# Layer 1's last two token blocks: seven block products for 12 of 16 inner slices, and a joined sign in the first weight steps

## The chip, the cores and the metric

The kernel runs on one core of one Trainium2 chip. The time is device microseconds of one execution. TensorE (PE) does the matmuls, VectorE (DVE), ScalarE (ACT) and GpSimd (POOL) the rest, and SyncE (SP) issues most DMAs.

## What is computed

Three independent things in one launch: an attention over 4 x 8 heads with 576 tokens (a coarse part over groups of four tokens and a local part under a band mask), and two layers over 2304 tokens each, chained so that the attention's output feeds layer 1 and layer 1's output feeds layer 2:

```python
out = out_up + out_local                     # attention, 2304 tokens x 512
h = np.maximum(x @ w_in, 0.0)                # layer 1: w_in 512 x 2048
y = h * h @ w_out                            #          w_out 2048 x 512
h = x @ w_in                                 # layer 2
g = np.maximum(h, 0.0) + np.log1p(np.exp(-np.abs(h)))
y = g @ w_out
```

All values are float32. PE is fed values rounded to a shorter format, so every operand is kept as a high part and a rest (`xh`, `xl` for the input, `gh`, `gl` for the activation, the two halves of `w` for the weights), and a product is three matmuls: high by high, high by rest, rest by high.

## The kernel before

**Tiles and steps.** Tokens come in five blocks of 512, 384, 384, 512 and 512. The inner dimension of 2048 is cut into 16 slices of 128. A step is (layer, block, slice): its hidden part is 12 matmuls (four pieces of the input dimension by three products) into a bank `ph` (L1315), the activation runs on ACT (`activate`; for layer 1 `Relu` and `Square`, L1328 and L1331; for layer 2 `Abs`, `Exp`, `Ln` on ACT and one DVE instruction, L1339), DVE and ACT split it into `gh` and `gl`, and the output part is 12 matmuls into four banks `y` (L1389), which collect all slices of a block.

**Order of the steps.** `RUNS` lists them by (layer, block, slices). Blocks 0 to 2 go through both layers while the attention of later blocks is still computed beside them. Then come `(0, 3, ALL), (0, 4, ALL[::-1])`, layer 1 of blocks 3 and 4, with a plain hidden part for each, and at last layer 2 of these two blocks, in another form.

**Seven products.** In layer 2 the hidden parts of blocks `ONE` = 3 and `TWO` = 4 for two slices are computed together as a 2 x 2 block product (Strassen's scheme): the two halves of the input dimension, the two slices, the two blocks. `fast_hidden` issues seven products `p` of 6 matmuls each (L1258) where the plain form has 4 x 12 = 48. The scheme needs sums of inputs (`token_sums`, `more_sums`, `last_sums`, split into `tt` or into block `TWO`'s own `xh`, `xl` by `t_split`), sums of weights (`weight_sums`: two sums `wf` of 512 columns, four of 256, one cast and two rests `ws` per pair), and sums of products (`keep_sum` copies a bank to `sum` on ACT, `add_sum` adds a bank to it on DVE at L1285, which also frees the bank). The banks that hold products are two of the ring `r_h` and two of the ring `r_a`. Block `TWO`'s activations are kept in `stash` until its outputs run.

**Weights.** Eight slots hold a slice's weights. The first time, SP loads raw words (`raw<-wts`, a ring of three) and `weight_job` (L425 to L462) turns 8-byte words into high part and rest: ACT takes the absolute value (L433), the low limb (L437) and the signed high limb (L439), DVE shifts and masks (L444), adds (L447, `f<-f,r`), one of both casts, and DVE takes the rest (L375). A slice needed again is loaded ready-made from `wdram` by POOL (L477).

**What sets the order.** The kernel is built by a planner: each strand of work is a generator that yields an engine, a duration and the events it needs, and the class `Order` always issues the one that can start first, with an urgency to break ties. What an engine does is then in that fixed order. Where the planner sees PE idle in the first part, `idle` matmuls on `ident` (L1068) are issued as fillers.

Of the kernel before, what the change touches and what calls it, by code (L numbers as in the profile page):

```python
# [44 lines left out]
LOW, HIGH = list(range(NF // 2)), list(range(NF // 2, NF))  # L45
ALL = LOW + HIGH
KEEP = 5
RUNS = [(0, 0, LOW), (0, 1, ALL), (0, 0, HIGH), (1, 1, HIGH), (1, 0, HIGH + LOW), (1, 1, LOW[:KEEP]),
        (0, 2, ALL), (1, 1, LOW[KEEP:]), (1, 2, LOW[KEEP:] + HIGH + LOW[:KEEP]),
        (0, 3, ALL), (0, 4, ALL[::-1])]  # L50
XBUF = [0, 1, 0, 1, 0]
ONE, TWO = 3, 4
PAIRS = [(f, f + 1) for f in range(0, NF, 2)]
# [18 lines left out]
UNIT_STEPS = [[0, 0] for _ in PAIRS]  # L72
for i, fs in ((ONE, [(0, 0), (1, 0), (0, 1), (1, 1)] + [(u, k) for u in range(2, len(PAIRS)) for k in range(2)]),
              (TWO, [(u, k) for u in reversed(range(len(PAIRS))) for k in (1, 0)])):
    FIRST[i + NB] = start = len(STEPS)
    for u, k in fs:
        if i == ONE:
            UNIT_STEPS[u][k] = len(STEPS)
        halves = ((0, 256), (256, 256)) if i == TWO and (u, k) == fs[-1] else ((0, 512),)
        for t0, n in halves:  # L80
            RUN_OF.append((start, PAIRS[fs[-1][0]][fs[-1][1]]))
            STEPS.append((1, i, PAIRS[u][k], t0, n))
    LAST[i + NB] = len(STEPS) - 1
FAST_TWO = FIRST[TWO + NB]
# [14 lines left out]
OUTS = 4  # L99
# [11 lines left out]
def plan_weights():  # L111


    uses = [lay * NF + f for lay, _, f, _, _ in STEPS]
    held, fills, fill_of, used = {}, [], [], {}
    for s, c in enumerate(uses):
        if c not in held:
            free = [i for i in range(SLOTS) if i not in held.values()]
            if free:
                held[c] = free[0]  # L120
            else:
                near = uses[max(0, s - (5 if s >= FAST else 3)):s]

                def worth(x):
                    return -min(uses.index(x, s) if x in uses[s:] else len(uses), s + NF + 1), used[held[x]]

                old = min((x for x in held if x not in near), key=worth)
                held[c] = held.pop(old)
            fills.append((s, c, held[c], used.get(held[c])))
        used[held[c]] = s  # L130
        fill_of.append(max(i for i, x in enumerate(fills) if x[1] == c))
    return fills, fill_of
# [39 lines left out]
class Ring:  # L172
# [10 lines left out]
    def take(self, name):  # L183
        b = Event()
        b.tile, b.free = self.make(name), None
        self.taken.append(b)
        return b

# [115 lines left out]
def fused_kernel(ctx: ExitStack, tc: tile.TileContext, lq, lk, lv, dqk, dv, cdmask, pqk, pv, pvn, wts, cmask, cident, out):  # L304
    nc = tc.nc
    act, dve, pe, sp = nc.scalar, nc.vector, nc.tensor, nc.sync
    const = ctx.enter_context(tc.tile_pool(name="const", bufs=1))
# [12 lines left out]
    ident = const.tile([128, 128], F32, name="ident")  # L320
    fours = const.tile([128, 32], F32, name="fours")
    placed = const.tile([128, 224], F32, name="placed")
    mask = const.tile([128, 3, KW], F32, name="mask")
    ident16 = const.tile([128, 128], BF16, name="ident16")
    mask16 = const.tile([128, 3, KW], BF16, name="mask16")
# [4 lines left out]
    r_r = ring(prep, "r", [128, 512], 2, I32)  # L330
    r_xh = [ring(main, f"xh{k}", [128, NP, NMAX], 1, F32R) for k in range(2)]
    r_xl = [ring(main, f"xl{k}", [128, NP, NMAX], 1, F32R) for k in range(2)]
    r_part = ring(prep, "part", [128, NMAX], NP)
# [63 lines left out]
    jobs = [(i, half) for i in range(len(fills)) for half in range(2) if half or fills[i][0] < FAST_TWO]  # L397
# [27 lines left out]
    def weight_job(j):  # L425
# [11 lines left out]
        act.activation(out=limbs[:, :, 0], in_=low, func=AF.Copy, scale=2.0 ** -13)  # L437
        t = yield "act", t_act(512)
        act.activation(out=limbs[:, :, 1].bitcast(I16), in_=high.bitcast(F32), func=AF.Prelu,  # L439
                       scale=2.0 ** -19, alpha=2.0 ** 60)  # L440
        raw.free = t
# [3 lines left out]
                          op0=ALU.logical_shift_left, op1=ALU.bitwise_and)  # L445
        t = yield "dve", t_dve(512)
# [17 lines left out]
    def slot_free(j):  # L464
        (_, _, slot, old), half = fills[j[0]], j[1]
        needs = [lent[slot]] if slot in lent else []
        if old is not None:
            needs.append((hidden_done, out_done)[half][old])
# [611 lines left out]
    whole, two_y = events(NP), events(NP)  # L1080
    plain = {(i, m): Event() for i in (ONE, TWO) for m in range(NP)}
    t_ready = {(n, kk): Event() for n in range(1, 5) for kk in range(2)}
    stashed = {x: Event() for x in range(NF)}

    def open_late():
# [10 lines left out]
        late.at = 0.0  # L1096
        for kk in range(2):
            order.spawn(token_sums(kk), FAST - 30)
        for u in range(len(PAIRS)):
            order.spawn(weight_sums(u), UNIT_STEPS[u][0] + U_WEIGHTS)  # L1100

    def pass_late(i, m, y):

        if i == TWO:
            two_y[m].buf = y
            yield None, 0.0
            two_y[m].at = order.free["pe"] + 0.1
            return
        t = yield either, t_either(512), late, late_ring
        b = whole[m].buf = late.stash.take("xf")  # L1110
        copy(b.tile, y.tile)
        y.free = whole[m].at = t
        yield from plain_split(i, m, b.tile)

    def plain_split(i, m, x):

        t = yield either, t_either(512, i == ONE)
# [4 lines left out]
        plain[i, m].at = t + 0.1  # L1122
        if i == TWO:
            two_y[m].buf.free = t
# [7 lines left out]
    def token_sums(kk):  # L1132

        t = yield "dve", t_dve(512), whole[kk], two_y[kk], late_ring
        t1 = late.stash.take("t1")
        dve.tensor_tensor(out=t1.tile, in0=two_y[kk].buf.tile, in1=whole[kk].buf.tile, op=ALU.subtract)
        two_y[kk].buf.free = t
        order.spawn(t_split(1, kk, t1), FAST - 28, t)
        order.spawn(more_sums(kk, t1), FAST - 26.5, t)

    def more_sums(kk, t1):

        t = yield "dve", t_dve(512), whole[kk + 2], two_y[kk + 2], late_ring
        t2, y = late.stash.take("t2"), two_y[kk + 2].buf
        dve.tensor_tensor(out=t2.tile, in0=y.tile, in1=t1.tile, op=ALU.subtract)
        order.spawn(t_split(2, kk, t2), FAST - 24, t)
        order.spawn(plain_split(TWO, kk + 2, y.tile), FAST - 19, t)
        order.spawn(last_sums(kk, t2), FAST - 20, t)

    def last_sums(kk, t2):  # L1150

        for n, op in ((3, ALU.subtract), (4, ALU.subtract)):
            t = yield "dve", t_dve(512), late_ring
            b = late.stash.take("t3")
            x, y = (t2, whole[kk].buf) if n == 3 else (whole[kk + 2].buf, t2)
            dve.tensor_tensor(out=b.tile, in0=x.tile, in1=y.tile, op=op)
            order.spawn(t_split(n, kk, b), FAST - 21 if n == 3 else FAST - 18, t)
        whole[kk].buf.free = whole[kk + 2].buf.free = t

    def t_split(n, kk, b):  # L1160

        th, tl = t_tiles(n, kk)
        t = yield "act", t_act(512)
# [3 lines left out]
        t_ready[n, kk].at = b.free = t + 0.1  # L1167

    def weight_sums(u):

        s0, s1 = UNIT_STEPS[u]
# [21 lines left out]
        s_ready[u].buf = b  # L1193
        s_ready[u].at = t + 0.1

    s_ready, ending = events(len(PAIRS)), events(2)
# [9 lines left out]
    def fast_hidden():  # L1206

        order.late = True
        units = [Event() for _ in PAIRS]
        for u, x in enumerate(units):  # L1210
            x.copied, x.added = events(3), Event()
            x.sums = [None] * 3
        seq = [(u, p) for ps in ((1, 2), (5,), (6,), (7,), (4,), (3,)) for u in range(2) for p in ps] + [(2, 1)]
        for u in range(2, len(PAIRS)):
            seq += [(u, 2), (u, 6), (u, 5), (u, 7)] + [(u + 1, 1)] * (u < len(PAIRS) - 1) + [(u, 4), (u, 3)]
        first, second = ([x.tile for x in x_tiles[i].buf] for i in (ONE, TWO))
        for u, p in seq:
            x, (s0, s1) = units[u], UNIT_STEPS[u]
            w0, w1 = (weights[fills[fill_of[s]][2]][:, 0] if w_ready[fill_of[s], 0].at is not None else None
                      for s in (s0, s1))  # L1220
            ones = [plain[ONE, kk + 2 * (p == 2)] for kk in range(2)]
            needs = {1: [r_h, w_ready[fill_of[s0], 0], *ones], 2: [r_a, w_ready[fill_of[s0], 0], *ones],
                     6: [x.copied[0], s_ready[u], t_ready[2, 0], t_ready[2, 1]],
                     5: [r_a, s_ready[u], t_ready[1, 0], t_ready[1, 1]],
                     7: [x.copied[1], s_ready[u], t_ready[3, 0], t_ready[3, 1]],
                     4: [x.copied[2], w_ready[fill_of[s1], 0], t_ready[4, 0], t_ready[4, 1]],
                     3: [x.added, s_ready[u], plain[TWO, 2], plain[TWO, 3]]}[p]
            if (u, p) == (1, 1):
                needs.append(out_done[FAST - 1])
            t = yield "pe", 6 * t_pe(512), *needs  # L1230
            w0, w1 = (weights[fills[fill_of[s]][2]][:, 0] for s in (s0, s1))
            if u == len(PAIRS) - 1 and p in (3, 7):
                ending[p == 3].at = t - 0.1
            if p == 1:
                x.long = r_h.take("p1")
                hidden_at[s0].at = hidden_at[s1].at = t
            elif p == 2:
                x.b = r_a.take("p2")
            elif p == 5:
                x.d = r_a.take("p5")  # L1240
            bank = {2: x.__dict__.get("b"), 5: x.__dict__.get("d"), 3: x.__dict__.get("d")}.get(p, x.long)
            prs = []
            for kk in range(2):
# [3 lines left out]
                else:  # L1247
                    k = SUMS[{6: 2, 5: 1, 7: 3, 3: 4}[p]] + kk * 128
                    a, c = (s_ready[u].buf.tile[:, half, k:k + 128] for half in range(2))
# [11 lines left out]
            if p in (1, 6, 7):  # L1261
                order.spawn(keep_sum(x, (1, 6, 7).index(p)), s0 - 20 if u > 1 else FAST - 29, at)
            if p == 2:
                order.spawn(add_sum(x, 0, x.b, s0, None, True), s0 - 20 if u > 1 else FAST - 27 + u, at)
# [339 lines left out]
```

## Time and profile before

| | us |
|---|---|
| median of 3 runs | 887.42 (886.86 to 889.75) |
| profiled execution | 886.4 |
| its span, first to last instruction | 884.6 |
| busy: PE, DVE, ACT, POOL | 875.5, 660.1, 508.5, 80.9 |
| layer 1, blocks 3 and 4 | 539.19 to 712.67 |
| layer 2's phase of seven products | 712.67 to 829.05 |
| outputs of the last block | 829.05 to 880.7 |

Times in rows are counted from the span's start. A matmul's duration in a row is longer than its share of PE's time, since matmuls overlap in the pipeline; what counts is the distance from one start to the next. The same holds for DVE and ACT.

### The profile page before, as it was taken

To read this page: it belongs to the slowest core of one execution; us is meant where nothing else is said; L and a number is where in the kernel's file an instruction comes from. 1 tells how busy PE (TensorE), PEld (TensorE's weight loads), DVE (VectorE), ACT (ScalarE), POOL (GpSimd) and SP (SyncE) were. 2 spreads that over 40 slices of the span, in tenths; PEclk is the share of its full clock that TensorE was granted. 3 is DMA by queue.
4 is the path that set the end of the run, shared out by engine and by line. 5 is a ranking of instruction groups with operands and counts; after the bars stand their busy time and mean duration, and the time that the engine had idled before them with its cause. 6 is when DMAs were issued, how large, how long until landed. Compare 5 with 4: busy or idle time off the path is not lost.

```text
span 884.6 us, 13257 instructions
## 1 busy us (share of the span) xinstructions
PE 875.5 (99%) x4844; PEld 751.9 (85%) x4844; DVE 660.1 (75%) x1169; ACT 508.5 (57%) x1092; POOL 80.9 (9%) x157
## 2 busy tenths in 40 slices
PE   8999999999999999999999999999999999999998
PEld 6888799998888888899999998888888888888786
DVE  7897878989999999998999999522322667775643
ACT  4998878778888984544445454222322366676500
POOL 0000000000000000122221221110011201100010
PEclk9999999999999999999999999999999999999999
DMA  9699679858976873898986998640266636320161
GB/s 298 224 319 329 202 255 331 295 170 304 319 231 206 291 265 96 265 331 285 299 293 195 311 304 256 209 136 0 72 190 191 191 118 191 115 76 1 38 201 47
DMA packets 51420, 186.82 MB, mean 211 GB/s; under 512 B 5778, under 2 KB 6418, under 8 KB 51228
## 3 DMA queue, kind: packets, MB, share of 16 engines
q1 hardware_dynamic: 29612, 107.20, 35.5%
q0 software_dynamic: 21600, 78.65, 28.7%
q8 instruction: 38, 0.62, 0.3%
q14 instruction: 26, 0.21, 0.1%
q10 hardware_dynamic: 144, 0.13, 0.0%
HBM read 147.69 MB, written 38.27 MB: 210 GB/s over the span
## 4 chain that ended last, share of the span: by engine, by line
PE 88%; DVE 7%; ACT 3%; issue 1%; DMA 1%; DVEq 0%; ACTq 0%
PE y L1389 40%; PE ph L1315 31%; PE p L1258 8%; PE idle L1068 1%; PE lsc L882 1%; DVE prod L986 1%; DVE do L1029 1%; DVE dsc L993 1%; DVE prod L1022 1%; PE psc L797 1%; DVE gl L375 1%; PE lpp L916 1%; DMA raw<-wts 1%; PE lav L926 1%; DVE do L1044 1%
## 5 line engine op out<-in xcount | busy, mean ns | idle before, releaser
L1315 PE MATMUL ph<-xh,w 128*128 128x384 f32 (+2 forms) x1040 | 311.1, 361 | 0.5 <-DVE g L1339 0.5
L1315 PEld LDWEIGHTS ph<-xh,w 128*128 128x128 f32 x1040 | 191.7, 188 | 22.8 <-issue 1.2
L1389 PE MATMUL y<-gh,w 128*128 128x512 f32 (+2 forms) x640 | 193.4, 364 | 0.0
L1315 PE MATMUL ph<-xl,w 128*128 128x512 f32 (+2 forms) x520 | 187.0, 360 | 0.0
L1389 PE MATMUL y<-w,gh 128*128 128x512 f32 x576 | 179.4, 392 | 0.0
L477 POOL DMA_DIRECT2D w<-wdram x150 | 79.8, 533 | 769.7 <-DVE gl L375 336.9
L1328 ACT ACTIVATE g<-ph 128x512 f32<-128x512 f32 (+2 forms) x82 | 44.5, 542 | 150.9 <-PE ph L1315 150.9
L1389 PEld LDWEIGHTS y<-gh,w 128*128 128x128 f32 x640 | 118.0, 188 | 14.1 <-issue 0.4
L1389 PEld LDWEIGHTS y<-w,gh 128*128 128x128 f32 x576 | 106.7, 188 | 21.4 <-issue 0.8
L364 DVE CAST gh<-g 128x512 fp32r<-128x512 f32 (+2 forms) x72 | 29.6, 412 | 127.5 <-PE y L1389 122.9
L1389 PE MATMUL y<-gl,w 128*128 128x512 f32 (+2 forms) x320 | 116.2, 363 | 0.2 <-DVE gl L375 0.2
L1389 PE MATMUL y<-w,gl 128*128 128x512 f32 x288 | 112.7, 391 | 0.3 <-DVE gl L375 0.3
L375 DVE TENSOR_TENSOR gl<-g,gh 128x512 fp32r<-128x512 f32 (+2 forms) x162 | 101.7, 628 | 12.8 <-ACT gh L362 9.9
L1315 PEld LDWEIGHTS ph<-xl,w 128*128 128x128 f32 x520 | 97.7, 188 | 10.6
L362 ACT ACTIVATE gh<-g 128x384 fp32r<-128x384 f32 (+2 forms) x90 | 50.6, 564 | 55.7 <-DVE g L1339 32.8
L1389 PEld LDWEIGHTS y<-gl,w 128*128 128x128 f32 x320 | 60.1, 188 | 7.9 <-DVE gl L375 1.2
L1389 PEld LDWEIGHTS y<-w,gl 128*128 128x128 f32 x288 | 54.0, 188 | 12.0 <-DVE gl L375 0.7
L437 ACT ACTIVATE r<-raw 128x512 uint16<-128x512 uint16 x64 | 50.2, 789 | 0.6 <-DVE f L447 0.6
L439 ACT ACTIVATE r<-raw 128x512 int16<-128x512 f32 x64 | 50.0, 786 | 0.0
L1022 DVE TENSOR_TENSOR prod<-dv,dsc 128x896 f32<-128x896 f32 x44 | 47.9, 1088 | 0.7
L1331 ACT ACTIVATE g<-g 128x512 f32<-128x512 f32 (+2 forms) x82 | 47.3, 577 | 1.7
L986 DVE TENSOR_TENSOR prod<-dqk 128x896 f32<-128x896 f32 x44 | 47.8, 1085 | 0.4
(172 smaller groups left out, 1190.6 us busy)
## 6 DMA issues: line engine op xcount, KB each, us to landing
w<-wdram POOLq DMA_DIRECT2D x150, 512.0 KB, 4.6
raw<-wts SPq DMA_DIRECT2D x64, 512.0 KB, 5.6
wdram<-w SPq DMA_DIRECT2D x64, 512.0 KB, 6.8
dqk<-dqk SPq DMA_DIRECT2D x11, 896.0 KB, 6.9
dv<-dv SPq DMA_DIRECT2D x11, 640.0 KB, 6.7
in<-pqk SPq DMA_DIRECT2D x12, 579.0 KB, 12.4
out<-o SPq DMA_DIRECT2D x17, 256.0 KB, 5.7
pv<-pv SPq DMA_DIRECT2D x12, 288.0 KB
```

The source lines that it names most:

```text
L362: act.activation(out=out, in_=in_, func=AF.Copy)
L375: dve.tensor_tensor(out=out, in0=whole, in1=high.bitcast(F32), op=ALU.subtract)
L437: act.activation(out=limbs[:, :, 0], in_=low, func=AF.Copy, scale=2.0 ** -13)
L439: act.activation(out=limbs[:, :, 1].bitcast(I16), in_=high.bitcast(F32), func=AF.Prelu, scale=2.0 ** -19, alpha=2.0 ** 60)
L477: nc.gpsimd.dma_start(out=weights[slot][:, half], in_=wdram[c, half])
L986: dve.tensor_tensor(out=p4, in0=k4[:, :, tok:tok + TAPS, :], in1=q4[:, tok].unsqueeze(2).to_broadcast([128, 2, TAPS, D]), op=ALU.mult)
L1022: dve.tensor_tensor(out=p4, in0=v4[:, :, :, tok:tok + TAPS], in1=s4[:, tok].unsqueeze(2).to_broadcast([128, 2, D, TAPS]), op=ALU.mult)
L1258: pe.matmul(bank.tile, w, y, start=(k == 0 and p in (1, 2, 5)), stop=(k == len(prs) - 1), skip_group_check=True)
L1315: pe.matmul(ph.tile[:, :n], w, y, start=(k == 0), stop=(k == len(prs) - 1))
L1328: act.activation(out=o, in_=h, func=AF.Relu)
L1331: act.activation(out=o, in_=o, func=AF.Square)
L1389: pe.matmul(o, wt, y, start=(begin and k == 0), stop=(end and k == 2))
```

## The change

In layer 1, blocks 3 and 4 first run slices 0 to 3 alone in the plain form (`ALONE`), block 3's part sum is copied out of the banks (`keep_part`), and the other 12 slices run as six pairs with seven products. `fast_hidden` and its helpers take a phase as argument (`PHASES`: layer 1 with six pairs, layer 2 with eight as before). `ONE` is now block 4 and `TWO` block 3, in both layers. The input in full, which the sums need, is made from `xh + xl` (`again_whole`). In layer 2's phase the products use the four banks `y`, and block `ONE`'s outputs the others. Block 3's kept part sums are added to its new ones on the way into layer 2 (`add_kept`, `less_whole`). In the weight steps needed by the first 12 steps (16 jobs: eight slices, two halves) ACT makes one instruction less and DVE joins the sign by one more. The output ring has 3 tiles instead of 4, and some tiles move to other pools.

```diff
+ALONE = ALL[:4]
-        (0, 3, ALL), (0, 4, ALL[::-1])]
+        (0, 3, ALONE), (0, 4, ALONE[::-1])]
+ONE, TWO = 4, 3
-ONE, TWO = 3, 4
...
+PHASES = [Phase(0, [f for f in ALL if f not in ALONE]), Phase(1, ALL)]
...
-OUTS = 4
+JOINED = 12
+OUTS = 3
...
-        act.activation(out=limbs[:, :, 0], in_=low, func=AF.Copy, scale=2.0 ** -13)
-        t = yield "act", t_act(512)
-        act.activation(out=limbs[:, :, 1].bitcast(I16), in_=high.bitcast(F32), func=AF.Prelu,
-                       scale=2.0 ** -19, alpha=2.0 ** 60)
-        raw.free = t
+        joined = fills[j[0]][0] < JOINED
+        if joined:
+            act.activation(out=r.tile, in_=low, func=AF.Copy, scale=2.0 ** -13)
+        else:
+            act.activation(out=limbs[:, :, 0], in_=low, func=AF.Copy, scale=2.0 ** -13)
+            t = yield "act", t_act(512)
+            act.activation(out=limbs[:, :, 1].bitcast(I16), in_=high.bitcast(F32), func=AF.Prelu,
+                           scale=2.0 ** -19, alpha=2.0 ** 60)
+            raw.free = t
...
+        if joined:
+            t = yield "dve", t_dve(512)
+            dve.scalar_tensor_tensor(out=fu, in0=high, scalar=0x80000000, in1=fu,
+                                     op0=ALU.bitwise_and, op1=ALU.bitwise_or)
+            raw.free = t
...
+    def again_whole(ph, m):
+
+        for i, to in ((ONE, ph.whole), (TWO, ph.other)):
+            t = yield "dve", t_dve(512), x_ready[i], late_ring
+            b = to[m].buf = late.stash.take("x")
+            xh, xl = (y.tile[:, m, :].bitcast(F32) for y in x_tiles[i].buf)
+            dve.tensor_tensor(out=b.tile, in0=xh, in1=xl, op=ALU.add)
+            to[m].at = t + 0.1
...
+    def add_kept(ph, m, y):
+
+        t = yield "dve", t_dve(512), halves_kept[m]
+        b = ph.other[m].buf = halves_kept[m].buf
+        dve.tensor_tensor(out=b.tile, in0=y.tile, in1=b.tile, op=ALU.add)
+        y.free = ph.other[m].at = t
+        order.spawn(plain_split(ph, TWO, m, b.tile), ph.base + 11, t)
+
+    def less_whole(ph, kk):
+
+        t = yield "dve", t_dve(512), ph.whole[kk], halves_kept[kk]
+        b = ph.less[kk].buf = halves_kept[kk].buf
+        dve.tensor_tensor(out=b.tile, in0=b.tile, in1=ph.whole[kk].buf.tile, op=ALU.subtract)
+        ph.less[kk].at = t
...
+        r_long, r_two = (Both(r_y[:2]), Both(r_y[2:])) if lay else (r_h, r_a)
...
-        yield from fast_hidden()
+        for ph in PHASES:
+            yield from fast_hidden(ph)
...
+                    if x == TWO and not ph:
+                        stream = keep_part(halves_kept[m], ys[m], w, None)
```

On PE, in layer 1 of blocks 3 and 4, a part of the order before is this (`xh`, `xl` a block's input, `w_...` the slice's weights in their slot):

```order
L1389 MATMUL y_6141<-gl,w_890 128x512
L1389 MATMUL y_6141<-gh,w_890 128x512
L1315 MATMUL ph<-xh,w_1495 128x512
L1315 MATMUL ph<-xl,w_1495 128x512
L1315 MATMUL ph<-xh,w_1495 128x512 x2
L1315 MATMUL ph<-xl,w_1495 128x512
L1315 MATMUL ph<-xh,w_1495 128x512 x2
```

On PE, in the same stage, after the first products of two pairs, it is now this (`tt` sums of inputs, `ws` sums of weights, each `p_...` a bank):

```order
L1497 MATMUL y_6323<-gl,w_1125 128x512
L1497 MATMUL y_6323<-gh,w_1125 128x512
L1363 MATMUL p_6435<-tt,ws 128x512 x6
L1363 MATMUL p_6456<-tt,ws 128x512 x6
L1363 MATMUL p_6435<-tt,ws 128x512 x6
L1363 MATMUL p_6456<-tt,ws 128x512 x6
L1363 MATMUL p_6435<-tt,w_1362 128x512 x6
L1363 MATMUL p_6456<-tt,w_1530 128x512 x6
```

A block's hidden part of 12 matmuls per slice has given way to products of 6 for both blocks.

On DVE, where the last attention task hands over block 4's input (`do`, then its split `xh`, `xl`), the order before goes on with nothing but the splits of activations:

```order
L1044 TENSOR_TENSOR do<-dpp,up 128x4x128
L364 CAST xh<-do 128x4x128
L375 TENSOR_TENSOR xl<-do,xh 128x4x128
L364 CAST gh<-g 128x512
L375 TENSOR_TENSOR gl<-g,gh 128x512
L364 CAST gh<-g 128x512
L375 TENSOR_TENSOR gl<-g,gh 128x512
```

At the same place on DVE it now goes on with the sums for the phase (`wf` sums of weights, `x` the input in full, `t_...` sums of inputs):

```order
L1102 TENSOR_TENSOR do<-dpp,up 128x4x128
L413 CAST xh<-do 128x4x128
L424 TENSOR_TENSOR xl<-do,xh 128x4x128
L1285 TENSOR_TENSOR wf<-w_943 128x512
L1179 TENSOR_TENSOR x<-xh,xl 128x512 x8
L1239 TENSOR_TENSOR t_6279<-x 128x512
L424 TENSOR_TENSOR gl<-g,gh 128x512
L1239 TENSOR_TENSOR t_6299<-x 128x512
L1285 TENSOR_TENSOR wf<-w_1362 128x512
L424 TENSOR_TENSOR xl<-t_6279,xh 128x512
```

The splits of activations stand between sums, in a row that goes on for some fifty instructions.

On DVE near the start, where weights of the first slices are prepared, the order before has one mask and one addition for a half slice:

```order
L444 TENSOR_SCALAR f<-f 128x512
L375 TENSOR_TENSOR xl<-lt,xh 128x4x64
L447 ISA f<-f,r 128x1024
L375 TENSOR_TENSOR xl<-lt,xh 128x4x64
L364 CAST w_87<-f 128x512
L375 TENSOR_TENSOR w_87<-f,w_87 128x512
```

There DVE now has the join at L501 between them, which reads `raw`:

```order
L424 TENSOR_TENSOR w_83<-f,w_83 128x512
L501 SCALAR_TENSOR_TENSOR f<-raw,f 128x512
L424 TENSOR_TENSOR xl<-lt,xh 128x4x64
L505 ISA f<-f,r 128x1024
L497 TENSOR_SCALAR f<-f 128x512
L803 TENSOR_REDUCE vd<-pv 72x256
L424 TENSOR_TENSOR w_84<-f,w_84 128x512
L501 SCALAR_TENSOR_TENSOR f<-raw,f 128x512
```

The signed limb has moved from ACT to DVE, and DVE is now the engine that releases `raw`.

## Rows read from the trace of the kernel before

**Rows 1.** The page, busy time, share and instructions of each engine.

```profile
PE 875.5 (99%) x4844; PEld 751.9 (85%) x4844; DVE 660.1 (75%) x1169; ACT 508.5 (57%) x1092; POOL 80.9 (9%) x157
```

**Rows 2.** The page, PE's busy tenths in 40 slices.

```profile
PE   8999999999999999999999999999999999999998
```

**Rows 3.** Windows from 539 us: window, length, busy (x) by engine, clock, DMA.

```profile
539.19:712.67 173.48, 173.01 (x765) 142.93 (x764) 66.77 (x115) 48.65 (x81) 25.52 (x48) 1.00 0.49 149
712.67:829.05 116.38, 115.89 (x511) 95.64 (x511) 80.82 (x138) 78.27 (x138) 9.82 (x18) 1.00 0.27 86
```

**Rows 4.** Windows of the start: PE, weight loads, DVE, ACT, POOL.

```profile
30.00:70.00 40.00, 39.04 (x418) 33.31 (x417) 38.15 (x99) 36.66 (x114) 0.00 (x0) 1.00 0.85 298
70.00:150.00 80.00, 79.68 (x578) 68.87 (x577) 62.67 (x140) 64.94 (x157) 0.00 (x0) 1.00 0.81 279
```

**Rows 5.** Windows of the fillers alone (L1068): PE and weight loads.

```profile
39.05:60.00 20.95, 3.37 (x22) 2.85 (x22) 1.00 0.78 264
60.00:125.00 65.00, 2.74 (x16) 2.15 (x16) 1.00 0.78 264
```

**Rows 6.** The chain from 700 us: start, length, what.

```profile
705.87 2.72 PE ph L1315 x12
...
718.11 12.24 PE p L1258 x54
```

**Rows 7.** Timeline of DVE at block 4's input: start, duration, instruction.

```profile
562.83 0.43 DVE L364 CAST xh<-do 128x512 fp32r<-128x512 f32 x1
563.29 0.69 DVE L375 TENSOR_TENSOR xl<-do,xh 128x512 fp32r<-128x512 f32 x1
```

**Rows 8.** Timeline of DVE within layer 2's phase.

```profile
739.90 0.70 DVE L364 CAST ws<-wf 128x1024 fp32r<-128x1024 f32 x1
740.51 0.69 DVE L1285 TENSOR_TENSOR sum<-p,sum 128x512 f32<-128x512 f32 x1
741.11 0.68 DVE L375 TENSOR_TENSOR gl<-g,gh 128x512 fp32r<-128x512 f32 x1
...
747.70 1.80 DVE L1185 TENSOR_TENSOR wf<-wf 128x256 f32<-128x256 f32 x4
...
753.77 0.42 DVE L1185 TENSOR_TENSOR wf<-wf 128x256 f32<-128x256 f32 x1
754.13 0.69 DVE L1285 TENSOR_TENSOR sum<-p,sum 128x512 f32<-128x512 f32 x1
```

**Rows 9.** Timeline of PE, a hidden group's first matmul.

```profile
564.26 0.39 PE L1315 MATMUL ph<-xh,w 128*128 128x512 f32 x1
```

**Rows 10.** Timeline of DVE, entry of layer 2's phase; in brackets idle and releaser.

```profile
714.06 0.69 DVE L1136 TENSOR_TENSOR t<-y,xf 128x512 f32<-128x512 f32 x1 [1.50 <-PE y L1418]
715.45 0.69 DVE L375 TENSOR_TENSOR xl<-t,xh 128x512 fp32r<-128x512 f32 x1 [0.70 <-ACT xh L362]
...
719.50 0.69 DVE L1285 TENSOR_TENSOR sum<-p,sum 128x512 f32<-128x512 f32 x1 [0.76 <-PE p L1258]
...
722.29 0.69 DVE L1285 TENSOR_TENSOR sum<-p,sum 128x512 f32<-128x512 f32 x1 [0.30 <-PE p L1258]
```

**Rows 11.** Groups by line and form, 0 to 125 us: busy, mean ns | idle.

```profile
L439 ACT ACTIVATE r<-raw 128x512 int16<-128x512 f32 x20 | 15.5, 782 | 0.0
...
L447 DVE CUSTOM_DVE_ANT_0 f<-f,r 128x1024 uint16<-128x1024 uint16 x20 | 13.7, 687 | 2.3 <-ACT r L439 1.4
```

**Rows 12.** The chain from 39 to 62 us.

```profile
47.65 0.68 ACT r L439
...
51.25 0.68 ACT r L439
...
51.95 6.01 DMA raw<-wts
```

**Rows 13.** Loads `w` on POOL, 539 to 712.67 us: time to landing.

```profile
DMA to landing us min/median/max: 3.4/3.7/6.6
```

**Rows 14.** Stores of `out`, whole run: time to landing.

```profile
DMA to landing us min/median/max: 2.0/5.7/9.4
```

## What I expect

> **What bounds the kernel now.** I read the busy shares first: TensorE (PE) is busy 875.5 of 884.6 us, VectorE (DVE) 75%, ScalarE (ACT) 57% [rows 1]. The slices say where PE is not: only the first of the 40, besides the last, is under nine tenths [rows 2]. Then the stages by windows. In layer 1's last two blocks (539.19 to 712.67) PE is busy 173.01 of 173.48 us while DVE works 66.77 and ACT 48.65; in layer 2's phase of seven products (712.67 to 829.05) it is 115.89 of 116.38 with DVE at 80.82 and ACT at 78.27; the granted clock is 1.00 in both, the upper level (2.4 GHz) [rows 3]. So from 539 us on a matmul taken away is time taken away, as long as the other two deliver. The start is another regime: from 30 to 70 us PE works 39.04 of 40 us, but DVE 38.15 and ACT 36.66 [rows 4]; PE looks full there partly because it runs filler matmuls on `ident`, 22 records (3.37 us) from 39 to 60 us and 16 (2.74 us) from 60 to 125 us [rows 5]; each filler is recorded as two. There every engine is near its end.
>
> **The change part by part.**
>
> A. *Matmuls removed.* Twelve slices of layer 1's blocks 3 and 4, in six pairs: a pair cost 2 slices x 2 blocks x 12 = 48 matmuls in `ph`, and costs 7 products x 6 = 42 in `p`. That is 6 x 6 = 36 matmuls of 512 columns fewer; the outputs `y` stay. In the chain of waits 54 matmuls of `p` took 12.24 us back to back, and 12 of `ph` took 2.72 [rows 6]: 226.7 ns each in both forms. So **A = -36 x 0.2267 = -8.16 us**, all on the path.
>
> The Trainium skill ("TensorE: Matmul & The Clock Gate", section "Back-to-back issue gap") gives about 131 ns for a 512-column matmul in a stream of weight loads and matmuls; by it A would be an estimate of -4.7 us. The trace disagrees with 226.7 ns, and the sum goes by the trace.
>
> B. *Entry of layer 1's phase.* Here DVE gets much new work in a short time. The phase needs block 4's input, which the last attention task delivers: `xh` at 562.83, `xl` at 563.29 [rows 7]; with 0.60 us to the next start DVE is free for the sums at 563.89. Then, in the new order, up to the sum that frees the bank of the second unit's fifth product, come 40 additions or splits of 512 columns, 11 of 256, one cast of 512 and one of 1024. DVE's pace where it does not wait, from start to start: 0.60 us for a 512-column sum (740.51 to 741.11), 0.61 for a cast of 1024 (739.90 to 740.51), 0.36 for a 256-column sum (753.77 to 754.13) [rows 8], 0.46 for a cast of 512 (562.83 to 563.29) [rows 7]. 40 x 0.60 + 11 x 0.36 + 0.46 + 0.61 = 29.0 us: the sum ends at 592.9. PE, which starts a `ph` group at 564.26 [rows 9], has eight groups of 2.72, four products of 1.36 and the first unit's fifth ahead of it: 564.26 + 21.76 + 5.44 + 1.36 = 592.8. A dead heat. Where four 256-column sums feed each other they took 1.80 us, 0.45 each [rows 8]; 11 x 0.09 = 1 us more at worst. From below the bound is 0 (PE cannot run ahead of its own stream). From above I take DVE's idle time at the same place of layer 2's phase, 1.50 + 0.70 + 0.76 + 0.30 = 3.3 us [rows 10], as if all of it came to stand before that sum. I take **B = +0.5** (0 to +3.3), close to the count.
>
> C. *The rest of that phase.* After the entry PE has 483 matmuls up to its end, 109.5 us. DVE has by count some 53 us of work beside them, and ACT two instructions for an activation (`Relu`, `Square`) where layer 2 has three. Layer 2's phase keeps PE full with DVE at 80.82 and ACT at 78.27 in 116.38 [rows 3]. **C = 0**; what would have to go wrong is a wait, not load.
>
> D. *The joined sign at the start.* 16 weight jobs lose one ACT instruction (`r<-raw`, L439, 782 ns) and gain one DVE instruction of 512 columns with two tensors in, for which the nearest row is `f<-f,r` at 687 ns [rows 11]: ACT -12.5 us, DVE +11.0 us. `raw` is now released by DVE, so SP's next load `raw<-wts` stands behind DVE's queue; the chain holds one such load, 6.01 us at 51.95 [rows 12]. For a gain speaks that two L439 of 0.68 us stand in the chain shortly before [rows 12], and that the new order holds 13 fillers up to the place of 125 us where the old holds 19. At 6.11 us for 19 [rows 5] six are worth 1.9 us. For a loss speaks that DVE is the fuller engine in just that window, where about eight of the joins lie. Ends: -5 us (most of the fillers' 6.11 gone) to +11.0 (every join on the path). I take **D = -0.5**: about three quarters of the six fillers' worth are given back by DVE. For the range I carry -3 and +3, for a rival +5.5, half the joins.
>
> E. *Entry of layer 2's phase.* The banks change places, and the kept halves of block 3 bring four more sums of 0.60 us, two of them ahead of the outputs' end. DVE had 3.3 us of idle there [rows 10], which covers the two that fall into it: **E = 0**; without that cover +1.2.
>
> F. *Edits costed at nothing.* Twelve fewer loads `w<-wdram` on POOL; those left land in a median of 3.7 us, 6.6 at most, in this stage [rows 13], while the shortest time in the new order between a slot's release and its use is seven `y` groups, 19 us. The output ring shrinks from 4 to 3: an `out<-o` lands in a median of 5.7 us [rows 14], and the copy that waits for one stands about 10 us of DVE work behind that DMA's issue. If this cover failed, by the longest landing of 9.4 us, DVE would stand some 4 us while PE works on from finished inputs, and PE would lose at most those 4 us. Tiles that move between pools cost no instruction.
>
> **Sum** against the profiled execution, 886.4 us: 886.4 - 8.16 + 0.5 + 0 - 0.5 + 0 + 0 = 878.2. The median of the runs is 1.0 us above the profiled run, so the forecast is **879.2 us**, a gain of 0.9%.
>
> **The rivals.** What a measurement of this kernel can tell from no change is about 0.3%, 2.7 us: under 884.8 is faster, over 890.1 slower.
>
> 1. *DVE paces the first 125 us.* All 16 joins lie on the path: 887.4 - 8.16 + 0.5 + 11.0 = 890.7, slower. It decides from 15 joins on (10.3 us). For it: DVE is 95% full from 30 to 70 us. Against it: DVE has 17 us free from 70 to 150 [rows 4], and ACT gets its 12.5 us back. Chance 0.04.
> 2. *Half of that.* Eight joins of 0.687 us: 887.4 - 8.16 + 0.5 + 5.5 = 885.2, no difference that can be told. Chance 0.09.
> 3. *The entry stalls.* DVE comes late by B's upper end, 3.3 us, and D stays: 882.0. Still faster. Chance 0.16.
> 4. *ACT paced the start.* With 12.5 us off ACT most fillers go, D = -5: 874.7. Chance 0.07.
> 5. *The change does not do what it says.* By count the new order has 36 matmuls fewer, so this could only lie in the time of one, and both forms run at one rate [rows 6]. I give it nothing.
>
> **How the numbers follow.** The forecast has 0.64. Faster: forecast, 3 and 4, 0.87; same: 2, 0.09; slower: 1, 0.04. The range begins at 875.0: the forecast with B at 0 and D at -3 is 876.2, and a little of rival 4 is taken in. It ends at 884.5: rival 3 is 882.0, and the forecast with D at +3 and B at +2 is 884.2. It leaves out 1, 2 and most of 4, 0.2 together.
>
> **What the profile after would show.** A: the stage from the first `ph` of block 3 to the entry of layer 2's phase is about 165.8 us long where it was 173.48, and a matmul of `p` there takes 226.7 ns. B: no idle of PE over 0.5 us before the fifth products of the first two units, released by `sum`. D: the first `ph` of block 3 at 538.7 us, within about 3 us; if it starts at 544 or later, rival 2 or 1 holds, and the chain before 125 us should show DVE's weight steps in place of ACT's. E: the phase of layer 2 as long as before, 116.4 us. The forecast is wrong if PE waits within layer 1's phase at another place than its entry, or if the start moves by more than 3 us.

## The result and the profile after

The changed kernel takes 877.19 us (median, 876.83 to 877.70), the kernel before 887.14 (886.68 to 889.75): a ratio of 0.9882 with a 95% interval from 0.9862 to 0.9902. That is faster by about 10 us where 8.2 were forecast (887.4 to 879.2), and it lies within the range of 875.0 to 884.5.

The two traces say where the time went. The page of the changed kernel, to be held against [rows 1, 2], has PE as full as before on less work, and DVE 57 us fuller:

```profile
PE 865.9 (99%) x4798; PEld 744.8 (85%) x4798; DVE 717.6 (82%) x1271; ACT 525.1 (60%) x1123; POOL 74.7 (9%) x145
...
PE   8999999999999999999999999999999999999998
```

Layer 1's last two blocks begin with a hidden matmul at 537.28 us, before at 539.19: the start gave **1.91 us**. The windows from there on (length first, then busy time of PE, weight loads, DVE, ACT, POOL, the clock) answer to [rows 3]:

```profile
537.28:704.83 167.55, 166.56 (x735) 137.23 (x734) 110.59 (x193) 71.47 (x124) 19.58 (x37) 1.00 0.39 125
704.83:819.98 115.15, 114.66 (x506) 94.39 (x505) 85.63 (x148) 79.48 (x138) 9.86 (x18) 1.00 0.27 85
819.98:871.63 51.65, 51.65 (x229) 42.46 (x227) 22.02 (x39) 5.49 (x9) 4.24 (x8) 1.00 0.34 106
```

The border between the first two is not quite the same place as before, since one more group of 6 products (1.36 us) now runs ahead of it; the sum of both is what counts: 282.70 us after 289.86, **-7.16**. The last window, 51.65, did not change. -1.91 - 7.16 = -9.07, and the spans differ by 9.0 (884.6 and 875.6). The other microsecond of the medians is that the profiled run of before was 0.7 us below its median, and that of the changed kernel 0.15 above.

The price of a matmul is as forecast; a row of the chain of waits has 54 of the new products:

```profile
598.70 12.24 PE p L1363 x54
```

12.24 / 54 = 226.7 ns, so 36 fewer are -8.16 us. What is missing to -7.16, 1.0 us, stands almost wholly at the entry of layer 1's phase. PE's timeline there:

```profile
590.66 0.39 PE L1363 MATMUL p<-xh,ws 128*128 128x512 f32 x1
591.60 0.50 PE L1363 MATMUL p<-xh,ws 128*128 128x512 f32 x1 [0.55 <-DVE sum L1390]
591.93 0.39 PE L1363 MATMUL p<-xl,ws 128*128 128x512 f32 x1
```

From 590.66 to 591.93 two matmuls take 1.27 us where two at full pace take 0.45: 0.82 us lost, in front of the second unit's fifth product, to `sum`. DVE's timeline on the way there, from block 4's input to that sum:

```profile
560.88 0.43 DVE L413 CAST xh<-do 128x512 fp32r<-128x512 f32 x1
561.34 0.69 DVE L424 TENSOR_TENSOR xl<-do,xh 128x512 fp32r<-128x512 f32 x1
562.12 0.69 DVE L1285 TENSOR_TENSOR wf<-w 128x512 f32<-128x512 f32 x1
562.73 4.90 DVE L1179 TENSOR_TENSOR x<-xh,xl 128x512 f32<-128x512 f32 x8
...
588.28 0.68 DVE L1390 TENSOR_TENSOR sum<-p,sum 128x512 f32<-128x512 f32 x1
588.88 0.68 DVE L1285 TENSOR_TENSOR wf<-w 128x512 f32<-128x512 f32 x1
589.59 1.35 DVE L1290 TENSOR_TENSOR wf<-wf 128x256 f32<-128x256 f32 x3
590.86 0.68 DVE L1390 TENSOR_TENSOR sum<-p,sum 128x512 f32<-128x512 f32 x1
```

DVE does not wait once between 562.12 and 591.5. The count gave 29.0 us from its being free (561.94 here) to the end of the sum's 0.60; it is 591.46 - 561.94 = 29.5. Ahead of the second sum stand a weight sum and three quarter sums of the third pair, which nobody needs yet.

At the start the windows answer to [rows 4], and those of the fillers alone to [rows 5]:

```profile
30.00:70.00 40.00, 39.94 (x427) 34.58 (x427) 38.35 (x98) 33.89 (x112) 0.00 (x0) 1.00 0.79 272
70.00:150.00 80.00, 79.47 (x597) 70.73 (x596) 71.97 (x156) 65.38 (x157) 0.00 (x0) 1.00 0.87 303
```

```profile
39.05:60.00 20.95, 3.15 (x20) 2.63 (x20) 1.00 0.78 261
60.00:125.00 65.00, 1.22 (x8) 1.12 (x8) 1.00 0.84 286
```

From 30 to 70 us ACT has 2.8 us less to do, PE stands 0.9 us less, and DVE is hardly busier than before; the joins show from 70 us on, where DVE goes from 62.67 to 71.97 us of 80 and still has room. The fillers cost 4.37 us instead of 6.11. Not all of this lasts: PE's list of waits from 195 to 300 us, empty in the kernel before, now has two for DVE, 0.9 us together.

```profile
PE ppp L888 <- DVE ppt L413: 0.5, 1, 0.5
PE ph L1420 <- DVE g L1445: 0.4, 1, 0.4
```

### The profile page after: what moved, and what is told of

It is laid out like the page before. It is cut to its first block, busy times and chain, and to the rows that moved or that the text cites. A ratio compares the mean times of both kernels' runs of the same rounds, so it can differ in the third digit from the quotient of the medians.

```text
span 875.6 us, 13197 instructions
## 1 busy us (share of the span) xinstructions
PE 865.9 (99%) x4798; PEld 744.8 (85%) x4798; DVE 717.6 (82%) x1271; ACT 525.1 (60%) x1123; POOL 74.7 (9%) x145
## 4 chain that ended last, share of the span: by engine, by line
PE 88%; DVE 9%; ACT 2%; issue 1%; DMA 0%; DVEq 0%
PE y L1497 41%; PE ph L1420 24%; PE p L1363 14%; PE idle L1126 1%; PE pqk L741 1%; PE lsc L940 1%; PE psc L855 1%; PE psc L762 1%; PE ppp L791 1%; PE y L1528 1%; PE ppo L815 1%; DVE prod L1044 1%; DVE x L1179 1%; PE lpp L974 1%; DVE gl L424 1%
## 5 line engine op out<-in xcount | busy, mean ns | idle before, releaser
L1420 PE MATMUL ph<-xh,w 128*128 128x384 f32 (+2 forms) x848 | 247.8, 355 | 0.9 <-DVE g L1445 0.9
L1420 PEld LDWEIGHTS ph<-xh,w 128*128 128x128 f32 x848 | 155.7, 188 | 15.2 <-DVE g L1445 1.7
L1420 PE MATMUL ph<-xl,w 128*128 128x384 f32 (+2 forms) x424 | 149.5, 353 | 0.0
L535 POOL DMA_DIRECT2D w<-wdram x138 | 73.5, 534 | 766.4 <-DVE do L1087 334.7
L411 ACT ACTIVATE gh<-g 128x384 fp32r<-128x384 f32 (+2 forms) x105 | 59.4, 566 | 66.6 <-DVE g L1445 33.7
L1420 PEld LDWEIGHTS ph<-xl,w 128*128 128x128 f32 x424 | 79.7, 188 | 6.8
L1434 ACT ACTIVATE g<-ph 128x384 f32<-128x384 f32 (+2 forms) x58 | 30.0, 518 | 56.5 <-PE ph L1420 54.1
L1390 DVE TENSOR_TENSOR sum<-p,sum 128x512 f32<-128x512 f32 x42 | 28.8, 687 | 32.9 <-ACT sum L411 24.3
L1087 DVE TENSOR_REDUCE do<-prod 128x128 f32<-128x896 f32 x44 | 47.5, 1081 | 0.7
L1441 ACT ACTIVATE g<-g 128x512 f32<-128x512 f32 (+1 forms) x80 | 47.0, 588 | 1.7
```

What stands on the lines that cost most here:

```text
L411: act.activation(out=out, in_=in_, func=AF.Copy)
L535: nc.gpsimd.dma_start(out=weights[slot][:, half], in_=wdram[c, half])
L1087: dve.tensor_reduce(out=o4[:, tok], in_=p4, axis=AX.X, op=ALU.add)
L1390: dve.tensor_tensor(out=b.tile, in0=bank.tile, in1=b.tile, op=ALU.add)
L1420: pe.matmul(ph.tile[:, :n], w, y, start=(k == 0), stop=(k == len(prs) - 1))
L1434: act.activation(out=o, in_=h, func=AF.Relu)
```

## Experiments at the start

The start is read from when the first hidden matmul of layer 1's last two blocks begins ("begins" below, 539.19 before and 537.28 in the changed kernel). From there to PE's last matmul every variant of the start in the changed kernel takes 334.3 to 334.4 us, so that the rest of the kernel does not blur it. The kernel before, run again beside each set of experiments, had medians from 886.71 to 887.74 us, so a difference of 1 us between sets needs no cause in the kernel.

**Without the joined sign.**

```diff
-JOINED = 12
+JOINED = 0
```

> The changed kernel without the joined sign: ACT makes three instructions for every weight half again. Theory (the joined sign gave the 1.9 us by which layer 1's last blocks begin earlier): their first hidden matmul moves from 537.3 back to about 539.2 us, time about 879.1. Rival (the smaller output ring and the moved tiles gave it): 537.3 and 877.2.

881.25 us (879.67 to 884.43), 4.1 above the changed kernel; begins at 542.62. So the joined sign is what gains at the start. But the profiled run, 1.3 us above that median, begins 3.4 us later than the kernel before, which has no joined sign either, where the expectation had the same start. The views of waits from 340 to 400 us name the place, DVE's first and then PE's (what waits <- for whom: us, times, longest), and the chain shows the store itself:

```profile
DVE o L413 <- DMA out<-o: 2.4, 1, 2.4
```

```profile
PE ppp L888 <- DVE dn L1059: 1.8, 1, 1.8
```

```profile
366.11 10.56 DMA out<-o
...
376.69 0.69 DVE o L413
```

DVE stood for an output tile, in a stage in which it is the full engine (58.4 of 60 us busy from 340 to 400 us in the kernel before), and PE behind it for 1.8 us. That is step F; it has its own runs below. The other 1.6 us of the 3.4 are not traced to a place.

**The kernel before with the joined sign alone**: the same edit in `weight_job` as in the change, nothing else.

> The kernel before with the joined sign alone, 12 steps as in the change. Theory: the first hidden matmul of layer 1's last blocks moves from 539.2 to about 537.3 us and nothing after it changes, time about 885.2. Rival (the joined sign pays only together with the rest): 887.1.

884.11 us (883.65 to 884.61), ratio 0.9962 to the kernel before (0.9947 to 0.9977), so -2.0 to -4.7 us by the runs; it begins at 537.44, 1.75 earlier than before. From there to PE's last matmul it is 341.51 us, before 341.54: nothing else moved. The joined sign is a gain by itself, and a larger one than forecast.

**8 and 28 joins instead of 16.**

```diff
-JOINED = 12
+JOINED = 6
```

> The changed kernel with the sign joined for the first 6 steps alone: 8 joins instead of 16. Theory (a join saves ACT's time first and costs DVE little until DVE is full): between none and 16, first hidden matmul of layer 1's last blocks at 538 to 541 us, time 878 to 880. Rival (16 were already too many for DVE): under 537.3 us and 877.2.

879.20 us (878.36 to 879.63), begins at 539.03: between none and 16.

```diff
-JOINED = 12
+JOINED = 24
```

> The changed kernel with the sign joined for the first 24 steps: 28 joins, DVE +8.2 us and ACT -7.9 us more. Theory (DVE has used up its room with 16): first hidden matmul of layer 1's last blocks at 539 to 543 us, time 879 to 883. Rival (DVE still has room): 536 to 537.3 us and 876 to 877.2.

876.32 us (875.74 to 877.05), begins at 537.03. The forecast of the theory that 16 joins had used up DVE's room is wrong; the rival's held. Twelve more joins cost nothing, and if they gain, it is too little to be told from 877.19. The window from 70 to 150 us has DVE barely fuller than with 16 and ACT 5 us freer:

```profile
70.00:150.00 80.00, 79.47 (x597) 70.72 (x595) 72.98 (x154) 60.36 (x151) 0.00 (x0) 1.00 0.82 289
```

DVE is no fuller because the planner made the order anew. The casts `w<-f` of the weights may run on either engine, and from 0 to 300 us DVE makes 21 of them instead of 30, ACT 36 instead of 26. DVE's groups by form in that stretch, with 16 joins and with 28:

```profile
L413 DVE CAST w<-f 128x512 fp32r<-128x512 f32 x30 | 12.6, 421 | 4.3 <-PE ph L1420 3.7 <-PE y L1497 0.3
```

```profile
L413 DVE CAST w<-f 128x512 fp32r<-128x512 f32 x21 | 8.9, 422 | 4.0 <-PE ph L1420 2.2 <-PE y L1497 1.6
```

In the whole run DVE has 2.2 us more to do with the twelve joins (719.8 after 717.6 us), not the 8.2 of the expectation. So this run shows that the joins can be placed, and not that DVE had 8 us of room.

**More work for DVE, more work for ACT, in the same order.** Two kernels repeat one instruction of each of the 16 weight jobs, without the planner being told.

```diff
-            dve.scalar_tensor_tensor(out=fu, in0=high, scalar=0x80000000, in1=fu,
-                                     op0=ALU.bitwise_and, op1=ALU.bitwise_or)
+            for _ in range(2):
+                dve.scalar_tensor_tensor(out=fu, in0=high, scalar=0x80000000, in1=fu,
+                                         op0=ALU.bitwise_and, op1=ALU.bitwise_or)
```

> The changed kernel with the joining instruction on DVE issued twice in a row in each of the 16 weight jobs (the same value twice), the order else the same: DVE +10.9 us in the first 150 us. Theory (DVE had room for 16 joins, but is close to its end): the first hidden matmul of layer 1's last blocks at 540 to 545 us, time 880 to 885. Rival 1 of the prediction in its pure form (DVE paces the start, each join on the path): 548.2 us and 888.1. Rival (DVE has slack there): at most 538.3 and 878.2.

885.51 us (883.92 to 886.93), begins at 545.13, just above the theory's range: of 10.9 us on DVE 7.9 came through.

```diff
-            act.activation(out=r.tile, in_=low, func=AF.Copy, scale=2.0 ** -13)
+            for _ in range(2):
+                act.activation(out=r.tile, in_=low, func=AF.Copy, scale=2.0 ** -13)
```

> The changed kernel with ACT's remaining limb conversion issued twice in a row in each of the 16 weight jobs, the order else the same: ACT +10.6 us in the first 150 us, about what the joined sign had taken off it. Theory (what was gained at the start is ACT's time): the gain is lost, first hidden matmul of layer 1's last blocks at 539.2 us or a little later, time 879 to 881. Rival (the gain comes from elsewhere, from fewer fillers): 537.3 and 877.2.

880.35 us (879.63 to 881.13), begins at 540.08: of 10.6 us on ACT 2.8 came through. The theory held: ACT's time is worth something at the start, about a quarter of what was added. What is taken off ACT after 70 us is worth less: with 28 joins layer 1's last blocks begin only 0.25 us earlier. The windows of the kernel with DVE's repeat, with the clock third from the end:

```profile
30.00:70.00 40.00, 37.99 (x400) 31.73 (x395) 39.13 (x100) 29.98 (x104) 0.00 (x0) 1.00 0.71 243
70.00:150.00 80.00, 76.02 (x567) 66.01 (x566) 72.34 (x157) 61.06 (x150) 0.00 (x0) 0.98 0.81 281
```

From 30 to 70 us DVE is at 39.13 of 40 us, and PE falls from 39.94 to 37.99. So DVE is close to its end there, as the prediction had it, but the first 16 joins, which the planner could place, did not reach it. The granted clock is 0.98 in the second window, so a part of the 7.9 us is matmuls at the lower level, and not DVE's work itself. Whether the planner would have placed the repeats as well was not tried.

## Experiments on the entry of layer 1's phase

**Four sums more in DVE's row**, in the same order.

```diff
-            dve.tensor_tensor(out=b.tile, in0=xh, in1=xl, op=ALU.add)
+            for _ in range(2 if i == ONE else 1):
+                dve.tensor_tensor(out=b.tile, in0=xh, in1=xl, op=ALU.add)
```

> The changed kernel with four of the eight additions of the input in full done twice (the same value twice) at the entry of layer 1's phase, the order else the same: DVE +2.4 us ahead of the sums that free the banks. Theory (PE waits there because DVE's row of sums ends late): the wait of PE at the second unit's fifth product grows from 0.8 by 2.4 to about 3.2 us, part of it before the first unit's; time about 879.6. Rival (the wait is a fixed latency from the product to its sum): unchanged, 877.2.

880.58 us (878.80 to 881.43). From the first hidden matmul to PE's last it is 337.25 us, in the changed kernel 334.38: +2.87 for 2.4 us of sums. PE's list of waits from 555 to 720 us now has three, two of them (at 573.0 and 585.4 us) already for the rest `gl` of an activation that stands behind the sums:

```profile
PE y L1498 <- DVE gl L424: 2.1, 2, 1.2
PE p L1364 <- DVE sum L1391: 0.7, 1, 0.7
```

DVE's row is the limit there, and the dead heat that the prediction counted was one. Where the wait stands was expected wrongly: most of it (2.1 of 2.8 us) comes earlier, through `gl`.

**The third and later pairs' weight sums held back** until both sums that free the banks are issued.

```diff
+        ph.entered = events(2)
...
+        if u > 1 and not ph.lay:
+            need += ph.entered
...
+        if k == 0 and s in (ph.units[0][0], ph.units[1][0]):
+            ph.entered[s != ph.units[0][0]].at = t
```

> The changed kernel with the weight sums of the third and later pairs held back until the first two bank-freeing sums are issued: on DVE two sums of 512 and three of 256 columns move behind them, some 2.5 us. Theory: PE's wait of 0.8 us at the entry goes, time about 876.4. Rival (it is only moved to a later product, whose weights now come late): 877.2.

876.05 us (875.84 to 877.71), ratio 0.9878 (0.9864 to 0.9893); from the first hidden matmul to PE's last 333.82 us, 0.56 less than in the changed kernel. DVE's timeline has the weight sums behind the second sum, and DVE now stands before it:

```profile
586.99 0.69 DVE L1393 TENSOR_TENSOR sum<-p,sum 128x512 f32<-128x512 f32 x1
589.38 0.43 DVE L413 CAST gh<-g 128x512 fp32r<-128x512 f32 x1 [1.70 <-ACT g L1442]
589.72 0.69 DVE L1393 TENSOR_TENSOR sum<-p,sum 128x512 f32<-128x512 f32 x1
```

PE has no wait in the list from 555 to 720 us any more. Of the 0.82 us some 0.3 stay. They are no longer for the sums: by the rows DVE's order has the cast `gh` ahead of the second sum, the cast waits 1.70 us for ACT's activation `g`, and the sum follows the cast at once. By the runs this kernel can't be told from the changed one.

**Six slices alone, five pairs.**

```diff
-ALONE = ALL[:4]
+ALONE = ALL[:6]
```

> The changed kernel with six slices alone and five pairs: six matmuls more (+1.36 us), and four groups of matmuls more, 10.9 us, for PE before the phase's entry. Theory (the wait is DVE against PE's remaining stream): no wait at the entry, 877.2 + 1.36 - 0.8 = 877.8. Rival (the wait belongs to the phase's form): 878.6.

877.25 us (877.19 to 877.96); from the first hidden matmul to PE's last 335.09 us, +0.71. Six matmuls more are +1.36, so 0.65 of the entry's loss is gone, and no wait is listed from 555 to 720 us. More of PE's own work ahead of the entry removes the wait, as the theory says.

**Two slices alone, seven pairs.**

```diff
-ALONE = ALL[:4]
+ALONE = ALL[:2]
```

> The changed kernel with two slices alone and seven pairs: six matmuls less (-1.36 us), but 10.9 us less work for PE before the phase's entry, while DVE's sums begin no earlier, since block 4's input comes from the last attention task. Theory: PE waits at the entry for 5 to 9 us, time 877.2 - 1.36 + 4 to 8 = 880 to 884. Rival (DVE's row of sums isn't the limit): 875.8.

900.05 us (898.54 to 902.57), ratio 1.0139: slower than the kernel before, and far beyond what was expected. From the first hidden matmul to PE's last it is 359.38 us, +25.0. The loss is at two places, and the expectation had neither. First, block 4's input is late for the plain slices already; PE's timeline:

```profile
551.77 0.53 PE L1094 MATMUL dpp<-ident,do 128*128 128x128 f32 x2
554.69 0.33 PE L1094 MATMUL dpp<-ident,do 128*128 128x128 f32 x1 [2.39 <-DVE do L1087]
556.94 0.47 PE L1094 MATMUL dpp<-ident,do 128*128 128x128 f32 x1 [1.92 <-DVE do L1087]
559.03 0.80 PE L1420 MATMUL ph<-xh,w 128*128 128x512 f32 x1 [1.61 <-DVE xh L413]
```

551.77 to 559.03 is 7.26 us for four small matmuls: PE has run out of work until the last attention task is done, and what DVE had to do for that task was the limit, not the sums. With the waits that follow, and a granted clock of 0.80 from 551 to 560 us, PE is some 12 us behind at the end of the entry. Second, layer 2's entry, from 713 to 760 us, loses 14 us more. The largest wait there (from the list of waits), and the window in which it falls, with the clock third from the end, are these:

```profile
PE y L1497 <- ACT gh L411: 6.5, 1, 6.5
```

```profile
712.00:740.00 28.00, 21.55 (x81) 16.85 (x80) 24.62 (x44) 12.44 (x22) 2.12 (x4) 0.82 0.32 105
```

PE stands, the granted clock falls to 0.82 in the window (to the lower level, 1.2 GHz, for a part of it), and the work after the wait is slower as well: by PE's timeline three matmuls from 733.89 take 1.28 us, 0.43 each instead of 0.227.

```profile
733.89 1.05 PE L1497 MATMUL y<-w,gh 128*128 128x512 f32 x2
734.74 0.63 PE L1497 MATMUL y<-w,gl 128*128 128x512 f32 x1
735.17 1.05 PE L1497 MATMUL y<-w,gh 128*128 128x512 f32 x2
```

DVE's timeline shows what came late: a copy of block 4's result, which this kernel makes at 711.05, just before the entry, and the changed kernel at 675.36, 30 us ahead of its entry.

```profile
711.05 0.68 DVE L413 COPY xf<-y 128x512 f32<-128x512 f32 x1
```

By the code the reason is a ring: the copies and the kept activations of block `TWO` share 16 tiles. Six pairs keep 12 activations and leave four tiles for the four copies; seven pairs keep 14 and leave two. The trace agrees: two of the four copies are made early here too, at 677.5 and 680.0 us, and two late, at 710.0 and 711.1; the changed kernel makes all four from 672.9 to 677.1. A larger ring was not tried.

## Experiments on the output ring

**The kernel before with three output tiles.**

```diff
-OUTS = 4
+OUTS = 3
```

> The kernel before with three output tiles instead of four. Theory: DVE waits 0.4 to 2.4 us for a store near 370 us, PE loses up to that, first hidden matmul of layer 1's last blocks at 539.2 to 541.5 us, time 887 to 889. Prediction's step F (cover by other DVE work): no such wait, 539.2 us, 887.1.

889.56 us (887.77 to 890.60), ratio 1.0027 (1.0017 to 1.0037), about +2.4 us. It begins at 540.48, 1.3 us later than before; DVE's list of waits from 330 to 420 us has the store:

```profile
DVE o L364 <- DMA out<-o: 0.5, 1, 0.5
```

The wait there is a half microsecond, so not all of the 1.3 is shown to be this. The rest is in the tail, which the expectation did not have: PE's last matmul ends at 881.96, 5.0 us before the span's end, and in the kernel before 3.9 us. The chain shows one store more, and a copy, behind the last halves:

```profile
882.47 0.44 DVE o L364
...
882.92 0.37 ACTq L1474
...
883.40 0.60 ACT o L362
```

The changed kernel does not pay that part, since its last block's stores use the `sum` tiles; its tail is 3.9 us.

**The late weight sums and a fourth output tile** for block 0's last store, taken from memory that the attention holds until it ends.

```diff
+    r_o0 = ring(att, "o0", [128, 512], 1)
...
-        r = late.s if i == TWO else r_o
+        r = late.s if i == TWO else r_o0 if i == 0 and m == NP - 1 else r_o
```

> The changed kernel with the later weight sums (as in the run with them alone) and with a fourth output tile for block 0's last store, taken from memory that is free until the attention ends. Theory (three output tiles make DVE wait 0.4 to 2.4 us for a store near 370 us, from run to run): no wait of DVE for a store there, no wait of PE for a sum at the entry, first hidden matmul of layer 1's last blocks at 536.0 to 536.8 us, time 875.5 to 876.0. Rival (that wait costs PE nothing): 876.1 as with the sums alone, or 1 us more.

876.16 us (875.58 to 876.84), ratio 0.9877 (0.9863 to 0.9892). Neither wait is in its lists, and it begins at 536.04 us, the earliest of all; but the run with the sums alone had happened to have no wait for a store either and began at 536.73. By the runs the two are one. What the three tiles cost the changed kernel stays open. In its own trace DVE waits 1.2 us for a store, PE lists no wait from 340 to 400 us, and it begins at 537.28, no later than the kernel before with the joined sign and four tiles (537.44).

## Why the prediction was nearly right

**A** held to the last digit: 226.7 ns, 36 matmuls, -8.16 us. The rate that [rows 6] give for either form was all it needed.

**B** was put at +0.5 with a dead heat at 592.8 and 592.9, and measured 0.8; the row's idle of 0.55 us is just over the 0.5 that the prediction's sign allowed. The count of DVE's row was 29.0 us, it took 29.5. Four more sums lengthen the wait and later weight sums or more slices alone shorten it, so the mechanism is shown, too. Rival 3 (3.3 us) had the right place and a size too large.

**C** and **E** held: PE lists one wait from 575 to 715 us, the one of B; the distances at layer 2's entry add 0.1 us, not 1.2.

**D** is the term that was mis-sized. It was put at -0.5, "about three quarters of the six fillers' worth are given back by DVE"; the step that failed is this giving back. By the profiles the start gained 1.9 us, by the runs with the joined sign put in alone 2.0 to 4.7. What the traces show DVE to give back is the 0.9 us of waits from 195 to 300 us, and with 28 joins, in another order, PE is full from 150 to 300 us. The prediction had the number right, about eight joins in the full window, and took them to be added there. The windows of the line of the joins in the changed kernel (busy time, count), and those of the weights' addition before and after, say otherwise:

```profile
30.00:70.00 40.00, 4.77 (x7) 1.00 0.79 272
```

```profile
30.00:70.00 40.00, 6.37 (x10) 1.00 0.85 298
```

```profile
30.00:70.00 40.00, 5.23 (x8) 1.00 0.79 272
```

Seven joins came into the window, and two of ten additions, with what goes with them, left it for the time behind 70 us, where DVE had 17 us free. The prediction had named this room as the reason against rival 1, and then not used it for the forecast. It also missed that the conversion that remains on ACT becomes shorter: 663 ns, where the one it replaces took 784 (groups by form, 0 to 125 us, of the changed kernel and of the kernel before):

```profile
L488 ACT ACTIVATE r<-raw 128x512 int32<-128x512 uint16 x16 | 10.5, 663 | 0.2 <-DVE f L505 0.2
L501 DVE SCALAR_TENSOR_TENSOR f<-raw,f 128x512 uint32<-128x512 uint32 x16 | 10.8, 684 | 0.1
```

```profile
L437 ACT ACTIVATE r<-raw 128x512 uint16<-128x512 uint16 x20 | 15.6, 784 | 0.0
```

With 16 x 0.12 us that is 1.9 us more off ACT, 14.4 in all. The price of DVE's join was right: 684 ns for 687.

**Rivals 1 and 2** are out for 16 joins, and the run with each join repeated shows the mechanism behind them to be real once DVE's work grows in a fixed order. **Rival 4** had the right sign: ACT did pace a part of the start, but it put D at -5, where the traces have -1.9 and the runs -2.0 to -4.7.

**F** failed in one piece, with both of its numbers. "The copy that waits for one stands about 10 us of DVE work behind that DMA's issue" was too much: it is 8.2 us in the changed kernel (362.96 to 372.37, less the wait of 1.20), and no more without the joined sign. And the store took longer than the 5.7 us of the median: about 9.4 us here, 10.56 without the joined sign. The timelines of SP and DVE in the changed kernel:

```profile
362.96 1.85 SPq L1600 DMA_DIRECT2D out<-o  x3
```

```profile
372.37 0.69 DVE L413 COPY o<-y 128x512 f32<-128x512 f32 x1 [1.20 <-DMA out<-o]
```

The prediction had the longest landing, 9.4 us [rows 14], before it and took the median for the forecast. In the changed kernel this cost PE nothing that its trace shows, so F's miss did not spoil the total.

By the traces, then, the sum missed by 0.9 us (-9.07 instead of -8.16): D by -1.4, and B, C and E together by +0.5 the other way. That the total came out closer than D did is luck.

## What to carry to other kernels

Count the row of a second engine up to the one instruction that the bound engine waits for, from starts and not from durations: 53 instructions came out within 0.5 us, and the same count says which work in the row can wait. Where work moves between two engines that are both over 90% full, look beyond the full window for where the order can place it, and at work that either engine can do, before giving the gain back. A ring that just fits is a bound of its own: a store's landing time is to be taken at its longest and not at its median, and a ring shared by two users fits only as long as neither grows.

## What the runs showed of the hardware

An activation on ScalarE that writes 512 values as every other 16-bit half took 784 ns, and the same conversion written as whole 32-bit words 663 ns. In the kernel with two slices alone a wait of PE of 6.5 us was paid for twice: the granted clock in the 28 us around it was 0.82, and matmuls after it started 0.43 us apart instead of 0.227. The changed kernel's wait of 0.8 us at the entry left the clock at 1.00 in the stage's window.
